# Four heads per attention step, transposed by VectorE into 32-row groups, in a fused attention and two-MoE kernel

## The chip, the cores and the metric

One core of one Trainium2 chip runs the whole program. The metric is the device time of one execution in microseconds (us); lower is better. The engines named below are TensorE (PE in the rows; PEld is its weight load), VectorE (DVE), ScalarE (ACT), GpSimd (POOL) and SyncE (SP), which only issues transfers here.

## The reference

Attention with a sigmoid in place of the softmax, then two feed-forward layers. All data are float32.

```
q, k, v: [4 batches, 12 heads, 448 positions, 64]
scores = q @ k.T / 8 - log(448);  attn = sigmoid(scores);  o = attn @ v
x  = o with heads side by side: [1792 tokens, 768]
x  = silu(x @ w_in) @ w_out                 # w_in 768x2048, w_out 2048x768
h  = x @ w_in2;  g = (a0+a1 h+a2 h^2+a3 h^3) / (1+|b0||h|+|b1|h^2+1e-6)
out = g @ w_out2                            # [1792, 768]
```

## The kernel before

Everything is one program, written in order by hand: each engine works through its own instructions in the order of the code and waits by semaphores for the others. A float32 product is made of three passes in a shorter format: each operand is split into a high part (a copy into that format, by ScalarE) and a low part (the rest, a subtraction by VectorE), and high x high, low x high and high x low are added up in PSUM. The attention comes first and takes the first 158 us; then the two feed-forward layers run, with their own loops, which the change leaves alone but for where the output rows go.

**Attention.** A step `i` is a pair of heads (24 steps, `NPT`); two steps `e` and `o = e+1` make a period, of which there are 12. The 448 keys are three and a half chunks of 128: chunks 0, 1 and 2 of each step are units of their own, and the half chunks of `e` and `o` share the unit `LAST`. For a step, `load_k` and `load_q` bring k and q; q comes in pieces of 128 bytes so that `attn_X`, VectorE's transpose of 32x32 blocks, gives head dimensions on the rows; k is put in order by GpSimd (`mix`) and transposed by TensorE (`attn_T`, four 128x128 transposes against `ident`). `attn_C` splits both: two ScalarE copies, two VectorE subtractions. `attn_QK` makes a unit's scores: three passes (six for `LAST`), each of two matmuls on 64 rows of the array, one for each head of the pair. `attn_S` is the sigmoid, one ScalarE instruction over 896 columns for both heads, out of one of three PSUM pairs of banks (`pairs`), which it gives back. `attn_AV` multiplies by v, two heads in two column halves of the array; the float32 operands are not split here, so each of its matmuls is two instructions. Its sums lie in the PSUM banks `hb[0]` and `hb[1]`, which `attn_E` copies out by VectorE once in a period; the next period's first `attn_AV` into a bank has to wait for that copy.

**What else runs in the attention.** In the same queues weights are converted (`conv(True)`, put at the end of the last quarter of eight periods, by `CONVS`): ScalarE's absolute value (L238), two VectorE operations that wait for it (L239, L240), and in the next quarter two more (`conv_rest`, L243 and L246). From the fourth period on a generator `operands0` makes three operands for the next stage in each period: a ScalarE copy (`split_later`), a GpSimd subtraction for some, and a VectorE subtraction at the next `flush()`.

**The end.** `second2` makes the output in 128-token tiles of 384 columns; `evict` adds up and `store` sends each to HBM in one transfer (the last in two, on two queues).

Of the kernel before, what the change touches and what calls it, by code (L numbers as in the profile page):

```python
# [11 lines left out]
F32 = mybir.dt.float32  # L12
# [35 lines left out]
def attention_moe_moe(ctx: ExitStack, tc: tile.TileContext, q, k, v, w_in1, w_out1, w_in2, w_out2, a, b2, out):  # L48
# [217 lines left out]
    qs, ks, vs = {}, {}, {}  # L266
    ld_p = [None]
    ks_t = []
    LO, HI = slice(0, D), slice(D, 2 * D)
    SQ = 32  # L270

    def rest_of(i):
        return HI if i % 2 else LO

    def load_by_key(src, t, i, eng_hi, eng=nc.sync):
        b, hp = divmod(i, NP)
        at_ = 0
        for part in (LO, HI):
            n = NCH if part == rest_of(i) else NCH - 1
            (eng_hi if part == HI else eng).dma_start(  # L280
                out=t[part, :, : n * D],
                in_=src[b, 2 * hp : 2 * hp + 2, at_ : at_ + n * D].rearrange("h (p c) d -> p h (c d)", c=n),
            )
            at_ += n * D

    def load_k(i):
        if i < NPT:
            ks[i] = ks_t[i % 4]
            load_by_key(k, ks[i], i, nc.scalar if i < 2 else nc.sync)

    def load_q(i):
        if i >= NPT:
            return
        b, hp = divmod(i, NP)
        t = qs[i] = ld_p[0].tile([P, S], F32, tag="qs", name=f"qs_{i}", bufs=3)
        for part in range(2 * D // SQ):
            j, e0 = divmod(part * SQ, D)
            (nc.scalar if i == 0 and part % 2 else nc.sync).dma_start(
                out=t[part * SQ : (part + 1) * SQ, :].rearrange("l (c d) -> l c d", d=SQ),
                in_=q[b, 2 * hp + j, :, e0 : e0 + SQ].rearrange("(c l) d -> l c d", l=SQ),  # L300
            )

    mixed, xq = {}, {}

    def mix(i):
        if i >= NPT:
            return
        t = ks.pop(i)
        u = mixed[i] = ld_p[0].tile([P, 2 * NCH * D], F32, tag="km", name=f"km_{i}", bufs=2)
        dst, src = u.rearrange("p (c h d) -> p h c d", c=NCH, h=2), t.rearrange("p h (c d) -> p h c d", c=NCH)  # L310
        if i:
            nc.gpsimd.tensor_copy(dst, src)
            return
        for h, eng in enumerate((nc.vector, nc.gpsimd)):
            eng.tensor_copy(dst[:, h], src[:, h])

    def load_v(i):
        if i >= NPT:
            return
        vs[i] = ld_p[0].tile([P, 2, NCH * D], F32, tag="vs", name=f"vs_{i}", bufs=4)  # L320
        load_by_key(v, vs[i], i, nc.gpsimd, nc.gpsimd)
# [12 lines left out]
    Q2 = 2 * 2 * S  # L334
    qst = Ring([xa_all[:, i * 2 * S : (i + 1) * 2 * S].rearrange("p (j s) -> p j s", j=2) for i in range(2)])
    k_at = [Q2 + PAD + i * 2 * BK for i in range(3)]
    kst = Ring([xa_all[:, i : i + 2 * BK].rearrange("p (j s) -> p j s", j=2) for i in k_at])

    hb = []
    st, at = {}, {}  # L340
# [7 lines left out]
    rows = (slice(0, D), slice(D, 2 * D))  # L348

    def attn_T(i, p=None):  # L350
        t = mixed.pop(i)
        pk = p if p is not None else pairs.get()
        o = p if p is not None else pk[:, 0, :]
        for c in range(NCH):
            nc.tensor.transpose(o[:, c * P : (c + 1) * P], t[:, c * P : (c + 1) * P], ident)
        return p, pk, o

    def attn_X(i):
        x = xq[i] = ld_p[0].tile([P, S], F32, tag="xq", name=f"xq_{i}", bufs=1)
        nc.vector.transpose(x, qs.pop(i))  # L360

    def attn_C(i, p, pk, o):
        k_, q_ = st["k", i], st["q", i] = kst.get(), qst.get()
        both = ((k_, o[:, :BK]), (q_, xq.pop(i)))
        for x, src in both:
            nc.scalar.copy(x[:, 0, :], src)
# [1167 lines left out]
```

## Time and profile before

| what | us |
|---|---|
| median of 3 runs | 1033.39 (1032.8 to 1034.83) |
| the profiled execution: time | 1035.44 |
| its span, first to last instruction | 1033.7 |
| the attention in it | 0 to 158.14 |
| one attention period (12 of them) | about 12.5 |

The profiled execution is one run; the difference of 1.7 us between its time and its span lies before the first and behind the last instruction. Busy time is the time in which an engine had an instruction running; for TensorE the ends of matmuls are modelled, so that a busy TensorE may still have small gaps.

### The profile page before, as it was taken

The numbers are of one execution on the slowest core, as the hardware profiler recorded it, in microseconds if no ns is written. First come the engines' busy times: TensorE is split into PE (matmuls) and PEld (weight loads), VectorE is DVE, ScalarE is ACT, GpSimd is POOL, SyncE is SP. The second block draws the span as 40 slices with busy tenths as digits, with TensorE's granted clock in tenths as the row PEclk, the third lists the DMA queues.
The fourth block names the chain that finished last, engine by engine and source line by source line (L and its number), as shares of the span: only waits on it lengthen the run. The fifth ranks groups of instructions, "written<-read, shape, count | busy, mean of one in ns | idle before, by whom it ended". The sixth has DMA issues, their size and how long they took to land.

```text
span 1033.7 us, 15953 instructions
## 1 busy us (share of the span) xinstructions
PE 1025.8 (99%) x5568; PEld 894.2 (87%) x5568; DVE 700.8 (68%) x990; ACT 651.7 (63%) x967; POOL 271.3 (26%) x242
## 2 busy tenths in 40 slices
PE   9999999999999999999999999999999999999998
PEld 6555558999999988999988888888999999999998
DVE  4588766878977666354545639889897968655761
ACT  6788786676777666354645668676768866444430
POOL 4335420000000000000000065878958922310000
PEclk9999999999999999999999999999999999999999
DMA  8988777878677766598979734666778869976641
GB/s 173 214 192 205 199 208 255 271 235 277 228 280 246 269 234 226 192 355 302 392 283 378 280 105 152 218 225 205 261 256 301 285 214 298 346 254 204 221 155 54
DMA packets 183504, 249.29 MB, mean 241 GB/s; under 512 B 57280, under 2 KB 136768, under 8 KB 183424
## 3 DMA queue, kind: packets, MB, share of 16 engines
q1 hardware_dynamic: 169504, 224.10, 66.5%
q10 hardware_dynamic: 11152, 17.36, 4.9%
q0 software_dynamic: 2768, 6.82, 2.6%
q8 instruction: 44, 0.72, 0.3%
q14 instruction: 36, 0.29, 0.1%
HBM read 164.60 MB, written 83.62 MB: 240 GB/s over the span
## 4 chain that ended last, share of the span: by engine, by line
PE 75%; DVE 15%; ACT 5%; issue 2%; DMA 2%; POOL 1%; SPq 0%; DVEq 0%; ACTq 0%; POOLq 0%
PE hp L1000 13%; PE acc L578 13%; PE hb L407 7%; PE pair L383 6%; PE acc L725 6%; PE acc L726 6%; PE acc L727 6%; PE hb L1000 5%; PE hb L578 5%; DVE sb L831 3%; DVE sb L829 3%; DVE sb L844 3%; DVE hb L845 3%; ACT sb L826 2%; PE hb L725 2%
## 5 line engine op out<-in xcount | busy, mean ns | idle before, releaser
L725 PE MATMUL acc<-xa_all,woH 128*128 128x512 f32 (+1 forms) x252 | 91.9, 365 | 0.0
L726 PE MATMUL acc<-xa_all,woH 128*128 128x512 f32 (+1 forms) x252 | 91.9, 365 | 0.0
L727 PE MATMUL acc<-xa_all,woL 128*128 128x512 f32 (+1 forms) x252 | 91.9, 365 | 0.0
L398 ACT ACTIVATE sb<-pair,nls 128x896 f32<-128x896 f32 x84 | 80.4, 1011 | 16.1 <-PE pair L383 16.0
L435 POOL TENSOR_TENSOR woL<-wif,woH 128x768 fp32r<-128x768 f32 x9 | 16.5, 1854 | 248.1 <-ACT woH L434 248.1
L827 POOL TENSOR_TENSOR sb<-sb 128x1024 f32<-128x1024 f32 (+1 forms) x32 | 69.7, 2178 | 39.0 <-ACT sb L824 39.0
L407 PE MATMUL hb<-sb,vs 128*64 128x448 f32 (+1 forms) x384 | 73.0, 554 | 0.0
L230 ACT ACTIVATE sb<-sb 128x768 f32<-128x768 f32 x48 | 43.1, 897 | 42.2 <-DMA w1i<-sb 22.7
L578 PE MATMUL acc<-xb,wr 128*128 128x448 f32 x315 | 66.9, 362 | 0.0
L918 POOL TENSOR_TENSOR sb<-sb 128x384 f32<-128x384 f32 (+1 forms) x43 | 52.7, 1231 | 52.4 <-DMA sb<-gk 50.5
L578 PEld LDWEIGHTS acc<-xb,wr 128*128 128x128 f32 x315 | 58.9, 187 | 4.7 <-issue 0.7
L800 PE MATMUL hp<-hx,woL 128*128 128x512 f32 (+1 forms) x168 | 60.7, 362 | 0.0
L798 PE MATMUL hp<-hx,woH 128*128 128x512 f32 (+1 forms) x168 | 60.7, 362 | 0.0
L799 PE MATMUL hp<-hx,woH 128*128 128x512 f32 (+1 forms) x168 | 60.7, 362 | 0.0
L798 PE MATMUL hp<-xa_all,woH 128*128 128x512 f32 (+1 forms) x168 | 60.7, 362 | 0.0
L799 PE MATMUL hp<-xa_all,woH 128*128 128x512 f32 (+1 forms) x168 | 60.7, 362 | 0.0
L800 PE MATMUL hp<-xa_all,woL 128*128 128x512 f32 (+1 forms) x168 | 60.7, 362 | 0.0
L232 DVE TENSOR_SCALAR sb<-sb 128x768 f32<-128x768 f32 x52 | 29.0, 558 | 43.3 <-ACT sb L230 43.0
L824 ACT ACTIVATE sb<-sb,absb 128x1024 f32<-128x1024 f32 (+1 forms) x32 | 36.4, 1139 | 33.5 <-DVE hb L845 33.2
L233 DVE SCALAR_TENSOR_TENSOR sb<-sb 128x768 int32<-128x768 int32 x48 | 46.0, 959 | 13.0 <-ACT sb L231 11.9
L829 DVE TENSOR_TENSOR sb<-hp,sb 128x768 f32<-128x768 f32 (+1 forms) x31 | 33.6, 1084 | 28.9 <-ACT sb L826 28.8
L725 PEld LDWEIGHTS acc<-xa_all,woH 128*128 128x128 f32 x252 | 47.3, 188 | 5.5
(259 smaller groups left out, 2795.0 us busy)
## 6 DMA issues: line engine op xcount, KB each, us to landing
sb<-in_moe_w_in_dram SPq DMA_DIRECT2D x30, 768.0 KB, 7.3
sb<-in_moe_w_out_dram SPq DMA_DIRECT2D x29, 768.0 KB, 6.9
gd<-sb SPq DMA_DIRECT2D x64, 224.0 KB, 3.0
wf<-w0i SPq DMA_DIRECT2D x28, 384.0 KB, 4.1
gk<-sb SPq DMA_DIRECT2D x28, 384.0 KB, 3.6
gk<-sb SPq DMA_DIRECT2D x15, 512.0 KB, 3.1
woL<-gk SPq DMA_DIRECT2D x25, 256.0 KB, 4.9
w1i<-sb SPq DMA_DIRECT2D x16, 384.0 KB, 5.6
```

Of the source, the lines that this page charges most:

```text
L398: nc.scalar.activation(t, p[:, :, :S], AF.Sigmoid, bias=nls, scale=QKSCALE)
L407: nc.tensor.matmul(hb[i_ % 2][j * D : (j + 1) * D, :S], vs[i_][part, j, c * D : (c + 1) * D], t[part, j], start=(c == 0), stop=(c == LAST),)
L578: nc.tensor.matmul(o, w_[:, w], x[:, i_, :], start=first and kk == 0 and n_ == 0, stop=kk == HK - 1 and n_ == 2, skip_group_check=not first,)
L725: nc.tensor.matmul(o, woH[c][:, w], x[:, 0, :w_], start=(c == 0), stop=False)
L726: nc.tensor.matmul(o, woH[c][:, w], x[:, 1, :w_], start=False, stop=False)
L727: nc.tensor.matmul(o, woL[c][:, w], x[:, 0, :w_], start=False, stop=(c == KF - 1))
L798: nc.tensor.matmul(o, wh[:, w], x[:, 0, :wd_], start=first, stop=False)
L799: nc.tensor.matmul(o, wh[:, w], x[:, 1, :wd_], start=False, stop=False)
L800: nc.tensor.matmul(o, wl[:, w], x[:, 0, :wd_], start=False, stop=last)
L827: nc.gpsimd.tensor_tensor(out=q_, in0=q_, in1=a_, op=ALU.mult)
L829: nc.vector.tensor_tensor(out=u1, in0=o, in1=u1, op=ALU.mult)
L1000: nc.tensor.matmul(o, a_, y[:, w_, :], start=kk_ == 0 and n_ == 0, stop=kk_ == HF - 1 and n_ == 2)
```

## The change

The attention takes two of the old steps at once. A step `x` (12 steps, `NQ`) is four heads, A the first two and B the last two. The pieces:

- `load_kq` brings k and q of four heads in one transfer each, 3584 contiguous bytes for every row: a row of SBUF holds 14 consecutive positions of one head, and each head has 32 rows. The order of tokens so becomes a permuted one, the same for all heads; `store` undoes it, with four transfers of 32 rows for each tile where there was one.
- `attn_X` transposes k and q by VectorE, six instructions for a step: for each half of the 64 head dimensions k's 384 and 64 columns and q's 448. Four heads then lie in four groups of 32 rows.
- `attn_C` copies the high parts: k by GpSimd, q by ScalarE. `attn_L` makes the low parts with four VectorE subtractions. TensorE's transposes, `mix` and their PSUM are gone.
- `attn_QK` makes two units at once, one of A and one of B: six rounds (three passes for each half of the head dimensions), each of four matmuls on 32 rows of the array that write four different banks. The half chunks of A and B share one PSUM pair over two turns; a short ScalarE read (`fence`) of it stands between.
- A step is four turns: scores of two units, sigmoids (2, 2, 1, 2 units), then `attn_AV` of units of the turn before (3 or 2 or 1 of them). In the first turn of step `x` the work for `x+1` is done: `attn_X` at its beginning, then `attn_C`, `attn_E` of `x-1`, `attn_L`, and the loads for `x+2`.
- At the end of the attention `hb` is a pool of its own that is closed, and the later pair of banks (`hpair`) is allocated again.

```diff
+    def load_kq(x):
+        if x >= NQ:
+            return
+        b, hq = divmod(x, H // HQ)
+        for nm, src in (("k", k), ("q", q)):
+            t = raw[nm, x] = ld_p[0].tile([P, NB * D], F32, tag="raw", name=f"{nm}_{x}", bufs=3)
+            a_ = src[b, hq * HQ]
+            for eng, part in ((nc.sync, slice(0, P)),) if x else ((nc.sync, LO), (nc.scalar, HI)):
+                n = part.stop - part.start
+                eng.dma_start(
+                    out=t[part, :],
+                    in_=bass.AP(a_.tensor, a_.offset + part.start * NB * D, [[NB * D, n], [1, NB * D]]),
+                )
...
+    KT, QT = wf[1], (s12f, s34f)
+
+    def attn_X(x):
+        if x >= NQ:
+            return
+        src_k, src_q = (raw.pop((nm, x)).rearrange("p (b x) -> p b x", x=D) for nm in "kq")
+        n = LAST * NCH
+        for h in range(2):
+            dims = slice(h * SQ, (h + 1) * SQ)
+            nc.vector.transpose(
+                KT[h][:, P:BK].rearrange("p (c g l) -> p g c l", c=LAST, g=NCH),
+                src_k[:, :n, dims].rearrange("p (g c) x -> p g c x", c=LAST),
+            )
+            nc.vector.transpose(KT[h][:, :D].rearrange("p (b l) -> p b l", l=SQ), src_k[:, n:, dims])
+            nc.vector.transpose(QT[h][:, :S].rearrange("p (b l) -> p b l", l=SQ), src_q[:, :, dims])
+
+    def attn_C(x):
+        if x >= NQ:
+            return
+        (kh, _), (qh, _) = parts[x % 2]
+        for h in range(2):
+            (nc.gpsimd.tensor_copy if x else nc.scalar.copy)(kh[:, h, D:], KT[h][:, :BK])
+            nc.scalar.copy(qh[:, h], QT[h][:, :S])
+
+    def attn_L(x):
+        if x >= NQ:
+            return
+        (kh, kl), (qh, ql) = parts[x % 2]
+        for h in range(2):
+            for src, hi_, lo in ((KT[h][:, :BK], kh[:, h, D:], kl[:, h, D:]), (QT[h][:, :S], qh[:, h], ql[:, h])):
+                nc.vector.tensor_tensor(out=lo, in0=src, in1=hi_.bitcast(F32), op=ALU.subtract)
+
+    last_of = {}
+
+    def attn_QK(x, *units):
...
+        for n, (a_, b_) in enumerate(((0, 0), (1, 0), (0, 1))):
+            for h in range(2):
+                for (s_, c), p in zip(units, ps):
+                    again = (x, c) in last_of
+                    at_ = M0 + c * P if c < LAST else D - s_ * D
+                    for j in range(2):
+                        r = slice((2 * s_ + j) * SQ, (2 * s_ + j + 1) * SQ)
+                        nc.tensor.matmul(
+                            p[:, j, :S],
+                            K[a_][r, h, at_ : at_ + P],
+                            Q[b_][r, h, :],
+                            start=(n == 0 and h == 0 and not again),
+                            stop=(n == 2 and h == 1),
+                            skip_group_check=again,
+                        )
+        for (s_, c), p in zip(units, ps):
+            if c == LAST and (x, c) not in last_of:
+                last_of[x, c] = p
+                nc.scalar.copy(fence, p[0:1, :, 0])
+            else:
+                at[x, s_, c] = p
+
...
-        dst = out[c0 : c0 + P, e0 : e0 + HM]
-        cut = HM // 2
-        if end:
-            nc.sync.dma_start(out=dst[:, :cut], in_=t[:, :cut])
-            nc.scalar.dma_start(out=dst[:, cut:], in_=t[:, cut:])
-        else:
-            nc.sync.dma_start(out=dst, in_=t)
+        for at_ in range(0, P, SQ):
+            b, r = divmod(c0 + at_, S)
+            dst = out[b * S : (b + 1) * S, e0 : e0 + HM].rearrange("(l b) e -> b l e", b=NB)[r // SQ]
+            eng = nc.scalar if end and at_ >= P // 2 else nc.sync
+            eng.dma_start(out=dst, in_=t[at_ : at_ + SQ, :])
 
...
+        A, B_ = 0, 1
+        SCORES = (((A, 0), (B_, 0)), ((A, 1), (B_, 1)), ((A, 2), (B_, LAST)), ((A, LAST), (B_, 2)))
+        READY = (SCORES[0], SCORES[1], ((A, 2),), ((A, LAST), (B_, 2)))
+        BEHIND = (((A, LAST), (B_, 2)), ((A, 0), (B_, 0)), ((A, 1),), ((B_, 1), (A, 2)))
+
+        for n in range(4 * NQ):
+            x, turn_ = divmod(n, 4)
             conv_outs()
+            if turn_ == 0:
+                attn_X(x + 1)
+            attn_QK(x, *SCORES[turn_])
+            attn_S(x, *READY[turn_])
+            of = x if turn_ else x - 1
+            if of >= 0:
+                for u in BEHIND[turn_]:
+                    attn_AV(of, *u)
+            if turn_ == 0:
+                attn_C(x + 1)
+                if of >= 0:
+                    attn_E(of)
+                    load_v(x + 1)
+                attn_L(x + 1)
+                load_kq(x + 2)
             flush()
             conv_rest()
+            if x >= NQ // B and turn_ != 2:
                 next(first_ops, None)
...
```

## Rows read from the trace of the kernel before

**Rows 1.** The page: span, busy time of TensorE, its granted clock in 40 slices
```profile
span 1033.7 us, 15953 instructions
...
PE 1025.8 (99%) x5568; PEld 894.2 (87%) x5568; DVE 700.8 (68%) x990; ACT 651.7 (63%) x967; POOL 271.3 (26%) x242
...
PEclk9999999999999999999999999999999999999999
```

**Rows 2.** Busy time by stretch (instructions), clock, DMA share: two periods, eleven together
```profile
32.43:44.93 12.50, 12.50 (x90) 6.77 (x90) 8.18 (x14) 9.53 (x13) 4.96 (x7) 1.00 1.04 237
82.47:95.09 12.62, 12.52 (x90) 6.80 (x90) 12.24 (x15) 10.30 (x16) 9.67 (x11) 1.00 0.77 195
19.95:158.14 138.19, 138.03 (x973) 73.98 (x973) 97.46 (x142) 109.62 (x150) 53.40 (x73) 1.00 0.84 205
```

**Rows 3.** The chain that ended last: start, length; second period, one whole, the end
```profile
19.95 2.01 PE pair L383 x18
...
43.27 1.65 PE hb L407 x8
44.93 2.01 PE pair L383 x18
46.94 1.82 PE hb L407 x12
48.75 1.41 PE pair L383 x12
50.16 0.59 PE pair L355 x4
50.75 2.40 PE hb L407 x12
...
154.82 3.32 PE hb L407 x20
158.14 9.33 PE acc L578 x45
```

**Rows 4.** Timeline where a period begins, at 82.47: start, length [idle before]
```profile
82.39 1.70 PEld L383 LDWEIGHTS pair<-xa_all 64*128 64x128 f32 x18 [0.70 <-ACT sb L398]
...
82.97 0.58 ACT L440 CAST xb<-xk 128x448 fp32r<-128x448 f32 x1
...
83.44 0.93 ACT L238 ACTIVATE sb<-sb 128x768 f32<-128x768 f32 x1
...
84.26 2.80 ACT L398 ACTIVATE sb<-pair,nls 128x896 f32<-128x896 f32 x3
84.39 0.56 DVE L239 TENSOR_SCALAR sb<-sb 128x768 f32<-128x768 f32 x1
...
84.99 1.38 DVE L240 TENSOR_SCALAR sb<-sb 128x768 int32<-128x768 int32 x1
85.30 0.21 PEld L407 LDWEIGHTS hb<-sb,vs 64*64 64x64 f32 x8 [0.70 <-issue]
...
86.38 1.15 DVE L420 COPY xk<-hb 128x448 f32<-128x448 f32 x2
```

**Rows 5.** Groups of VectorE in 82.47:95.09: count, busy us, mean ns, idle before
```profile
L360 DVE STREAM_TRANSPOSE xq<-qs 128x448 f32<-128x448 f32 x2 | 1.3, 630 | 0.0
L368 DVE TENSOR_TENSOR qx<-xq,qx 128x448 fp32r<-128x448 f32 x1 | 1.2, 1226 | 0.1
```

**Rows 6.** Timeline at the start: the first transpose and the first scores
```profile
6.49 0.65 DVE L360 STREAM_TRANSPOSE xq<-qs 128x448 f32<-128x448 f32 x1 [1.70 <-DMA qs<-in_q_dram]
...
7.79 1.74 PE L383 MATMUL pair<-xa_all 64*128 64x448 f32 x12 [0.15 <-ACT xa_all L366]
```

**Rows 7.** Timeline at the end: the stores of the last three tiles
```profile
1029.02 0.86 SPq L1043 DMA_DIRECT2D out_dram<-sb  x2
...
1030.46 0.33 SPq L1040 DMA_DIRECT2D out_dram<-sb  x1
```

**Rows 8.** DMA issues over the whole run: count, KB each, median us to landing
```profile
wif<-w1i SPq DMA_DIRECT2D x16, 384.0 KB, 5.4
out_dram<-sb SPq DMA_DIRECT2D x27, 192.0 KB, 2.2
```

More of the change, by code (lines that the diff above doesn't have):

```diff
@@ L286, in load_k @@
[L286 to L301, printed above, removed]
@@ L346, in warm @@
             nc.tensor.transpose(p[:, 1, :P], ident, ident)
[L348 to L366, printed above, removed]
-        for x, src in both:
-            nc.vector.tensor_tensor(out=x[:, 1, :], in0=src, in1=x[:, 0, :].bitcast(F32), op=ALU.subtract)
-        if p is None:
-            pairs.put(pk)
-    LAST = NCH - 1
-    def attn_QK(i, c):
-        p = pairs.get()
-        parts = [(i, ((0, 0), (1, 0), (0, 1)))]
-        if c == LAST:
-            parts.append((i + 1, parts[0][1]))
-        turns = [(i_, n) for i_, passes in parts for n in passes]
-        for n, (i_, (a_, b_)) in enumerate(turns):
-            K, Q = st["k", i_], st["q", i_]
+    M0 = P + D
@@ new lines, in attn_S, with attn_AV @@
+    def attn_S(x, *units):
+        for s_, c in units:
+            p = at[x, s_, c]
+            t = f2.get()
+            nc.scalar.activation(t, p[:, :, :S], AF.Sigmoid, bias=nls, scale=QKSCALE)
+            pairs.put(p)
+            at[x, s_, c] = t
+    seconds = {}
+    def attn_AV(x, s_, c):
+        t = at.pop((x, s_, c))
+        for w in (s_,) if c < LAST else (0, 1):
+            part = slice(0, P) if c < LAST else (LO, HI)[w]
+            n = seconds[x, w] = seconds.get((x, w), 0) + 1
@@ L1055, in attention_moe_moe @@
-        qst.put(ld_p[0].tile([P, 2, S], F32R, tag="qx", name="qx"))
-        ld_p[0].tile([P, 16], F32, tag="qxpad", name="qxpad")
-        for i in range(2):
-            load_k(i)
-            load_q(i)
-        for i in range(4):
-            nc.vector.memset(ks_t[i][rest_of(i + 1), :, LAST * D :], 0.0)
+        load_kq(0)
         constants()
-        warm(16)
-        mix(0)
+        open_parts()
+        warm(24)
+        load_v(0)
         attn_X(0)
-        attn_C(0, *attn_T(0, hb[0]))
@@ L1152, in attention_moe_moe @@
+            if at_half == -3:
+                prep_s12(0)
+            if at_half == -1:
+                prep_a22(0)
+            if n == 0:
+                conv_load()
+            if n == 3:
+                conv_load()
+            if n == 4:
+                coefficients()
+            if n == 12:
+                coefficients_abs()
+            if n in CONVS:
+                conv(True)
         for _ in first_ops:
             pass
-        for u in waiting:
-            attn_AV(*u)
-        attn_E(NPT - 2)
@@ L1157, in attention_moe_moe @@
-        attn_E(NPT - 1)
+        for u in BEHIND[0]:
+            attn_AV(NQ - 1, *u)
+        attn_E(NQ - 1)
         flush()
```

251 lines of the change are left out of this document (95 added, 156 removed).

## The prediction

> **What bounds the kernel now.** The page comes first: TensorE has work for 99% of the span and its clock was granted in full in all 40 slices [rows 1]. With an engine so full the question is where its time stands between matmuls, so next comes the table by stretches over the attention: eleven periods and the last one's remainder, 19.95 to 158.14, took 138.19 us with TensorE busy for 138.03, while VectorE (97 us) and ScalarE (110 us) had room and the DMA engines fell from a share of 1.04 to 0.77 without the period getting shorter [rows 2]. So transfers and ScalarE set nothing there; TensorE does. The third view is the chain of waits, which for one period is TensorE alone, one kind of matmul after another [rows 3]. There the reader can take a price list. Scores: 18 matmuls 2.01 us, 12 take 1.41, so a pair of matmuls, side by side on two halves of the rows, costs 0.20, and each group has 0.21 on top for the change of shape. Products with v: 8 instructions 1.65, 12 take 2.40, so 0.19 each and 0.15 on top; the group with the shared half chunk has 12, eight of them on quarters of the array, and takes only 1.82: four small tiles at once cost what two do. Transposes: 0.59 twice a period. The fourth view is the timeline at the start of a period with a weight conversion, where VectorE's order becomes visible [rows 4].
>
> **What TensorE saves.** Removed: the two groups of transposes, 2 x 0.59 = 1.18 a period. The scores keep their streamed columns if four matmuls on 32 rows run side by side: 24 passes of four instead of 24 of two, but in four groups instead of three: 4 x 1.41 = 5.64 against 2.01 + 1.41 + 2.01 = 5.43, since a group of 24 small matmuls is six passes as one of 12 was. The products with v are in four groups: 1.82 + 1.65 + 0.90 + 1.65 = 6.02 (0.90 is 4 x 0.19 + 0.15) against 1.65 + 1.82 + 2.40 = 5.87. A new period is 11.66, an old one about 12.5. From the beginning of the second period to the end of the attention: 11 x 11.66, plus 1.82 for the products left over, is 130.1 against 138.2. That is -8.1 us.
>
> The trace has no 32-row matmul. Its lower bound for a pass of four is the 0.20 of a pair; its upper bound comes from the weight loads, 18 in 1.70 us, 0.094 each [rows 4]: if four loads had to follow each other, a pass would last 0.38, and 288 passes would cost 288 x 0.18 = 52 us. I take 0.20, because pairs already load two weights in one pass and the four quarter tiles cost no more than two halves [rows 3].
>
> **What VectorE gets, and the new wait.** VectorE loses two transposes a period (0.63 each [rows 5]) and gets six: 1792 columns where it had 896. Two operations of 448 columns back to back take 1.15 with 0.62 for one [rows 4], so one adds 0.53; by columns six cost 4 x 0.53 = 2.1, by count 6 x 0.53 = 3.2. Two are only 64 wide, so I take 2.3. The four subtractions stay. Mean load goes from 8.9 to about 10.1 of 11.7: below TensorE's, but the place matters. All six stand at the head of the first turn, before `attn_E`, and the first product with v of the second turn writes `hb[0]`, which `attn_E` has to have copied. Reckoned from the first turn's beginning TensorE comes to that product at 1.41 + 1.82 + 1.41 = 4.64. Where VectorE is free at 0, six transposes end at 2.3, the copy waits for TensorE until about 3.3 at the worst, and nothing is lost. Where a conversion was put at the end of the turn before, VectorE's next two instructions wait for ScalarE's L238, which stands behind two sigmoids and, from the fourth period on, a copy. In the last turn scores end 1.65 before the next period; from there 0.15 to the sigmoid (an estimate from modelled ends), 2 x 0.90 for two sigmoids (three took 2.80 with 1.01 each), 0.47 for the copy (start to start of L440 and L238) and 0.93 for L238 make 1.70 after the new period's beginning. Then L239 and L240, 0.60 + 0.56: 2.86; the transposes: 5.16; the copy of `hb[0]`, 0.62 and a semaphore: 5.84. TensorE stands for 5.84 - 4.64 = 1.2. Seven conversions precede a first turn with transposes: five with the copy (1.2 each), two before it (0.7 each): 7.4. In the old order the copy of `hb` came straight behind L240, at 86.38, and had until 82.47 + 2.01 + 1.82 + 1.41 + 0.59 = 88.3 [rows 3, 4], which is why nothing shows before. Once in these conversions L240 ran 1.38 beside GpSimd; I add 0.8 for one of those. Sum +8.2. Below, it is 0 if the order does not bite; above, 3.2 for the transposes makes every stall 0.9 longer, 14.5 in all.
>
> **ScalarE, GpSimd, PSUM.** ScalarE gives k's high part to GpSimd, two copies less a period, and gets the short read `fence`; GpSimd does two copies as `mix` did. In the tightest turn ScalarE has two sigmoids, two copies of q and one for an operand, 2 x 0.90 + 3 x 0.47 = 3.2, against the turn's 1.41 + 1.82 of TensorE: it keeps up, and costs nothing while q is transposed in time. A pair of PSUM banks is wanted again 1.65 after the scores end, and the first sigmoid gives it back after 1.16: 0.5 of cover. Behind the waiting q copies stand the next sigmoids; in a turn with a conversion they move by the same 1.2 that TensorE stands, so the stall is not paid twice.
>
> **Transfers.** q's 128-byte pieces go, and SyncE issues 6 transfers a period where it issued 12: nothing, since TensorE was full at a DMA share of 1.04 and of 0.77 alike [rows 2]. v now waits for its buffer to the end of the first turn and is wanted a period later: covered by eight microseconds, and k and q of `x+2` likewise.
>
> **The start.** Four heads of k and q are 0.92 MB instead of half of it. A 384 KB load lands after 5.4 [rows 8]; I put q at 6.5, where the first q was before [rows 6]. Then: q's first half 0.65, k's and q's second halves 1.1, four subtractions 2.3, so the last pass of the first scores runs at about 10.7, the sigmoid frees a pair at 12.1, scores to 13.55, products to 15.2, then 1.41 + 0.90 + 1.41 + 1.65: the second period begins at 20.55, before at 19.95 [rows 3]: +0.6, between -1 and +4.
>
> **The stores.** SyncE gets 84 issues more, each some 0.35 (0.86 for two [rows 7]); sixteen at once hold its queue for 6 us, and the loads behind them are asked for 14 units of 1.6 to 2 us ahead, so they cost nothing; if that cover went, 6 us each time. At the very end the last tile's four transfers follow those of two earlier tiles on two queues: the last issue starts about 0.7 later, 48 KB land perhaps 0.2 sooner than 96: +0.5, between 0 and 1.
>
> **Sum.** -8.1 + 8.2 + 0.6 + 0.5 = +1.2. The profiled execution took 1035.44, 2.05 above the median of the runs; against the median the forecast is 1033.4 + 1.2 = 1034.6 us.
>
> **Rivals.** (a) *The conversions do not hold the copies up*: the stall is gone and -7.0 remains, 1026.4 us. For it: VectorE has a fifth of its time free, and five periods have no such stall. Against it: the order of code and the 1.70. It decides where the copy of `hb[0]` ends before 4.64. (b) *VectorE fills up.* A period with conversion and operands asks for 1.16 + 2.3 + 1.1 + 2.3 + 1.6 (three operand subtractions) + 1.8 (L243 and L246, by their 768 columns at 0.53 for 448) = 10.3 alone, but the fullest such period already took it 12.24 of 12.62 [rows 2], because operations beside GpSimd stretch: a subtraction took 1.23 where a like one is 0.62 [rows 5]. With 1.2 more it is 13.4 for 12.9. From there a backlog goes over into the next period's transposes; 0.5 to 1.2 in five periods is +3 to +6, 1039 us. The Trainium skill (GPSIMD Engine Reference, section 1, Specifications) says that GpSimd shares its SBUF access with VectorE's instructions that have two SBUF inputs. By that rule k's subtractions, which read PSUM and SBUF before and SBUF twice now, become open to it too, and the sum would be at this rival's upper end; the trace agrees for q's, at 1.23 against 0.62. (c) *TensorE's clock.* In the start TensorE has only six passes between 6.4 and 12.1. If its granted clock fell there to the lower level (1.2 GHz, half), the next scores and products, 1.41 + 1.65, would double: +3, 1037.6. Against it: nothing before shows a fall, but nothing before stood so long either. (d) *Passes of four are slower than pairs.* With 0.06 more, a third of the way to the bound above, 288 passes cost 17 us and the kernel ends at 1052; with loads in a row, 1086. For it: no row has four 32-row matmuls. Against it: quarter tiles at the price of halves. The Trainium skill (TensorE: Matmul & The Clock Gate, Part 3, Packing small matmuls) gives 3.07 times for four row tiles instead of four; by that a pass would be 4 x 0.20 / 3.07 = 0.26 and the cost 17.5.
>
> **How the numbers follow.** Forecast 0.37, its own range 1031 to 1037; (a) 0.27; (b) 0.20; (c) 0.08; (d) 0.08. A measurement of this kernel can tell about 0.2%, 2.1 us, from no change. Faster: (a) and the lower edge of the forecast, 0.30. Same: most of the forecast and the weakest of (a) and (b), 0.30. Slower: (b), (c), (d) and the forecast's upper edge, 0.40. The range takes half of (a) in and leaves out (d): 1027 to 1043.
>
> **What would show it.** The chain should have no transposes and a period without conversion of 11.7. The wait list should show TensorE's products with v waiting for VectorE's copies of `hb`, some 1.2 in five periods and 0.7 in two; if that line is short, (a) holds. Score groups of 24 should take 1.41; 1.75 or more is (d). The granted clock of 0 to 20 us decides (c). VectorE's busy time above 12.5 in a period, with waits of scores on its low parts, is (b). The forecast is wrong in its main step if the periods after a conversion are no longer than the others.

## The result, and the profile after

The changed kernel takes 1043.51 us, median of four runs (1041.82 to 1046.35); the kernel before, run beside it, takes 1034.11. The ratio is 1.0095, with a 95% interval of 1.0068 to 1.0122: slower by 9.4 us. The forecast was 1034.6 with a range of 1027 to 1043, so it lies outside, if only just. The profiled execution took 1041.82, the fastest of the four, against 1035.44 before: +6.4 us are there to be read in the trace. The other 3 us of the medians are not: 1.7 because the changed kernel's profiled execution is its fastest, 1.3 because that of the kernel before lies above its median.

The page of the changed kernel, to be laid beside [rows 1]:

```profile
span 1040.0 us, 16921 instructions
...
PE 1018.2 (98%) x6048; PEld 886.0 (85%) x6048; DVE 709.6 (68%) x1033; ACT 644.0 (62%) x957; POOL 269.2 (26%) x250
...
PEclk8999999999999999999999999999999999999999
...
DMA packets 140387, 249.34 MB, mean 240 GB/s; under 512 B 17296, under 2 KB 90960, under 8 KB 140304
```

The clock's first slice of 26 us is no longer full. The table of stretches shows where (each row: stretch, length, busy time of the engines, then granted clock, DMA share and GB/s):

```profile
6.00:8.00 2.00, 0.36 (x4) 0.12 (x2) 0.00 (x0) 0.62 (x1) 0.51 (x1) 1.00 0.99 280
8.00:10.00 2.00, 0.00 (x0) 0.00 (x0) 0.90 (x2) 0.22 (x1) 0.56 (x1) 0.81 0.82 165
10.00:18.00 8.00, 6.46 (x50) 4.07 (x52) 6.57 (x15) 4.85 (x8) 2.87 (x5) 0.50 0.72 181
...
25.63:37.31 11.68, 11.68 (x131) 5.92 (x130) 3.52 (x6) 7.70 (x11) 3.30 (x6) 1.00 0.46 120
37.31:49.58 12.27, 11.79 (x132) 5.93 (x130) 8.51 (x16) 8.59 (x12) 3.45 (x6) 1.00 0.52 131
```

From 6.4 to the first scores at 10.40 TensorE had nothing to do; its clock fell in that time, at 9.2, and was 0.50, the lower level, up to 19.5; of the eight microseconds in the table TensorE was busy for 6.46. The chain shows what that costs, the first three lines at the lower level and the last at the full one:

```profile
11.56 2.62 PE pair L409 x20
...
15.22 2.61 PE pair L409 x22
17.82 2.48 PE hb L440 x8
20.31 1.41 PE pair L409 x15
```

The second period begins at 25.63, where it began at 19.95. The last two rows of the table are the attention's steady state: a period without a conversion ahead of it takes 11.68, with TensorE busy throughout; one with a conversion 12.27, and later, with an operand's copy in ScalarE's queue as well, about 12.7. What stands between is in the list of TensorE's waits from 0 to 165 (total, times, longest), which before held nothing but 1.4 for the start and one wait of 0.2. L383 makes q's high part, L454 and L457 copy `hb`, and L420 is `fence`; the 1.4 of the start is still there and left out here, with one wait of 0.7 for a sigmoid:

```profile
PE pair L409 <- ACT xa_all L383: 4.5, 2, 4.0
PE hb L440 <- DVE xk L454: 3.9, 5, 1.1
PE hb L440 <- DVE sb L457: 2.8, 3, 0.9
PE pair L409 <- ACT ident L420: 1.8, 1, 1.8
```

And the chain of waits through one such period, where [rows 3] had TensorE alone:

```profile
61.23 1.00 ACT sb L428
62.23 0.45 ACT xb L474
62.69 0.80 ACT sb L238
...
63.51 0.57 DVE sb L239
...
64.10 0.56 DVE sb L240
64.66 0.49 DVE wf L370
...
66.39 0.53 DVE sf L375
66.91 0.52 DVE xk L454
...
67.48 1.72 PE hb L440 x8
```

Sigmoid, an operand's copy, the conversion's L238, its two VectorE operations, six transposes (2.25 us), the copy of `hb[0]`, and only then the product with v. Behind the start the attention has no transposes on TensorE any more.

**The ledger of the two profiled executions** (after less before): start of the second period +5.68; from there to the first matmul behind the attention (at 165.30 and 158.07) 139.67 against 138.12, +1.55; first feed-forward layer -1.62; from its end to the last matmul +0.04; from the last matmul to the end of the span +0.73. The sum is +6.38. The +0.04 is itself a sum: laid matmul by matmul beside the kernel before, the changed one gains another 2.0 up to 915 and loses 2.1 in one place at 920, to which experiment 4 comes.

### The profile page after: what moved, and what is told of

Read it like the earlier page. It is cut to its first block, busy times and chain, and to the rows that moved or that the text cites. A ratio compares the mean times of both kernels' runs of the same rounds, so it can differ in the third digit from the quotient of the medians.

```text
span 1040.0 us, 16921 instructions
## 1 busy us (share of the span) xinstructions
PE 1018.2 (98%) x6048; PEld 886.0 (85%) x6048; DVE 709.6 (68%) x1033; ACT 644.0 (62%) x957; POOL 269.2 (26%) x250
## 2 busy tenths in 40 slices
DMA packets 140387, 249.34 MB, mean 240 GB/s; under 512 B 17296, under 2 KB 90960, under 8 KB 140304
## 4 chain that ended last, share of the span: by engine, by line
PE 64%; DVE 18%; DMA 6%; ACT 6%; issue 4%; POOL 2%; SPq 1%; ACTq 0%; DVEq 0%; POOLq 0%
PE acc L612 14%; PE hp L1034 9%; PE acc L759 6%; PE acc L760 6%; PE acc L761 6%; PE hb L612 5%; PE pair L409 4%; PE hb L440 4%; PE hbpair L1034 3%; DVE sb L865 2%; DVE sb L878 2%; DVE sb L863 2%; DVE hbpair L879 2%; PE hb L759 2%; PE hb L760 2%
## 5 line engine op out<-in xcount | busy, mean ns | idle before, releaser
L440 PE MATMUL hb<-sb,vs 128*64 128x448 f32 (+1 forms) x384 | 76.4, 562 | 6.7 <-DVE xk L454 3.9
L440 PEld LDWEIGHTS hb<-sb,vs 128*64 128x64 f32 (+1 forms) x384 | 19.4, 136 | 42.5 <-issue 22.3
L233 DVE SCALAR_TENSOR_TENSOR sb<-sb 128x768 int32<-128x768 int32 x48 | 46.0, 959 | 13.1 <-ACT sb L231 11.7
```

The costliest lines, as they stand in the source:

```text
L440: nc.tensor.matmul(hb[w][j * D : (j + 1) * D, :S], vs[x][part, 2 * w + j, c * D : (c + 1) * D], t[part, j], start=(n == 1), stop=(n == NCH),)
```

## The experiments

The theory after the result: the start lost 5.7 us by q's late landing and by the fall of the clock that follows it, and the conversions' stalls took back what TensorE saved. The rivals were that VectorE is simply too full, that the stores cost time in the middle, and that the start is one of the two causes alone.

**1. Copies first.** `hb` is copied ahead of the transposes; the splitting for `x+1` goes to the second turn.

```diff
             if turn_ == 0:
-                attn_X(x + 1)
...
-                attn_C(x + 1)
                 if of >= 0:
                     attn_E(of)
                     load_v(x + 1)
-                attn_L(x + 1)
+                attn_X(x + 1)
                 load_kq(x + 2)
+            if turn_ == 1:
+                attn_C(x + 1)
+                attn_L(x + 1)
```

> In the changed kernel's trace the seven periods behind a conversion are 0.6 to 1.2 us longer than 11.68, and one more and a wait of 1.9 in the third turn add to 9.2 us in all. Theory order: these waits come from the six transposes standing ahead of the copies of hb in VectorE's queue. With the copies first, and the high and low parts in the second turn, the periods behind a conversion go to 11.7 to 11.9, the attention ends 6 to 9 us earlier (before 159.5 instead of 165.4), and the time falls by as much, to about 1036. Rival full: VectorE has more work than the period has time; then the waits only move, to the scores' low parts or to the fence, and the attention ends less than 3 us earlier. The start (second period at about 25.6) stays in both.

Measured: 1039.67 us, ratio 1.0052 (1.0032 to 1.0071). No product with v waits for a copy of `hb` any more. Six periods in a row from 26.20 to 96.40 take 11.68 to 11.72, conversions or not; the second of them, which took 12.27 in the changed kernel:

```profile
37.88:49.60 11.72, 11.72 (x131) 5.93 (x130) 9.18 (x16) 8.48 (x12) 4.12 (x6) 1.00 0.51 163
```

Five of the six have a conversion ahead of them, so these five stalls were the order's and not VectorE's amount of work. Then one of 15.5: scores wait for low parts (1.6 in two waits) behind a VectorE subtraction that took 3.71, and the granted clock is 0.50 from 99.7 to 103.1. Attention ends at 161.65 instead of 165.30, 3.7 us earlier where 6 to 9 were expected: the late stalls, with VectorE behind, are the rival's.

**2. Conversions two turns later.** The other way to part the two.

```diff
-        CONVS = (7, 11, 15, 19, 23, 31, 35, 43)
+        CONVS = (9, 13, 17, 21, 25, 33, 37, 45)
```

> The same conversions, each put two turns later (end of the second turn), and nothing else moved: the transposes still stand ahead of the copies of hb, but the conversion's two VectorE instructions, which wait for ScalarE, no longer stand ahead of the transposes. Theory order: the waits for the copies of hb vanish as in the first experiment, 6 to 8 us. Rival full: the same amount of VectorE work, so the waits stay or move, less than 3 us. A wait of the fence or of the sigmoids in the third turn, at most 0.5 each, would be new, since the conversion's ScalarE instruction now stands before the fence.

Measured: 1042.22 us, ratio 1.0069 (1.0054 to 1.0084). The list of waits of this kernel, 0 to 165:

```profile
PE pair L409 <- ACT xa_all L383: 3.6, 2, 2.9
PE pair L409 <- ACT ident L420: 2.2, 1, 2.2
PE hb L440 <- DVE sb L457: 1.8, 2, 1.2
```

The line for `xk` is gone, and the six periods from 25.64 to 95.89 take 11.68 to 11.76. So both orders remove the first five stalls, by different means. Of the next three one is shorter than in the changed kernel and two are longer: 12.96, 12.33 and 15.6 (there 12.67, 12.71 and 14.57), the last with VectorE busy for 13.08 of it and the clock at 0.50 from 133.0 to 136.4, behind a wait of 2.2 for `fence`. The attention ends at 162.0, 3.3 us earlier.

**3. The start, four times.** *q alone*: two raw buffers instead of three, so that k and q of the second step are asked for only when the first are transposed, and v of the first step held until then as well.

```diff
-            t = raw[nm, x] = ld_p[0].tile([P, NB * D], F32, tag="raw", name=f"{nm}_{x}", bufs=3)
+            t = raw[nm, x] = ld_p[0].tile([P, NB * D], F32, tag="raw", name=f"{nm}_{x}", bufs=2)
...
+        attn_X(0)
+        nc.gpsimd.tensor_copy(ident[0:1, 2:4], QT[0][0:1, 0:2])
         load_v(0)
-        attn_X(0)
```

> One part of the start alone: the first v and the second k are asked for only after the first q is transposed. In the changed kernel q's second half landed at 9.08, its first at 6.25. Theory late q: both halves land by about 6.5, the first scores begin at 7.5 to 8 instead of 10.4, and the second period begins at 21.5 to 23.5 instead of 25.6. Rival clock: if TensorE's granted clock still falls to 0.5 in the start, at least 2 us of that are not won, and the second period begins later than 23. Rival bandwidth elsewhere: v or the second k come so late that the second turn or the second period waits for them; then nothing is won.

*Warmer*: TensorE transposes `ident` 44 times ahead of the first scores.

```diff
-        warm(24)
+        warm(44)
```

> The other part of the start alone: 44 warming transposes instead of 24, so that TensorE is busy from 1.4 to about 10.5; loads as in the changed kernel. Theory clock: the granted clock stays at 1.0, the scores and products between 11.5 and 20 take 1.4 and 1.65 instead of 2.6 and 2.5, and the second period begins at 22.5 to 23.5 instead of 25.6; the runs lie closer together than the 1041.8 to 1046.4 of the changed kernel, with a mean clock of 1.0. Rival: the clock falls all the same, in the gaps between 10.5 and 14, and less than 1 us is won.

*Both, with filling*: q alone (the copy that holds v back now writes into another small tile), 32 transposes ahead, four after each of the first five passes of scores and six behind the last.

```diff
+                if fill_now and n + h < 3:
+                    warm(fill_now)
...
-        warm(24)
+        warm(32)
...
-            attn_QK(x, *SCORES[turn_])
+            attn_QK(x, *SCORES[turn_], fill_now=0 if n else 4)
+            if n == 0:
+                warm(6)
```

> Both parts of the start together: first v and second k asked for after the first q, 32 warming transposes, and more of them between the first scores' passes and behind them, so that TensorE never stands long. Theory start: the granted clock stays at 1.0 throughout, and the second period begins at 20 to 22 instead of 25.6, so the attention ends 3.5 to 5.5 earlier. Rival loads: the second q and the first v come too late in any order (2.3 MB are wanted in the first 14 us), and the second period does not begin before 23.

*Two raw buffers only*: the first line of *q alone*, with v asked for at once.

> The changed kernel with two raw buffers instead of three: k and q of the second item are asked for only when VectorE has transposed k and q of the first, and v of the first item is still asked for at once. In the changed kernel the ACT half of q landed 7.74 us after its issue, first scores at 10.40, second period at 25.63. Theory (the second item's k is what makes q late): the ACT half lands about 5.5 to 6 us after its issue, first scores near 8.5, second period near 23.5 to 24.5, and v is there for the first products, unlike in the run that held v back. Rival (v's many short pieces make it late): it still lands 7 us or more after its issue and the second period starts at 25 or later. In either case the end moves by no more than that: 1041 to 1043 against 1043.5.

| kernel | us, ratio (interval) | q's ACT half lands after | first scores | second period | granted clock |
|---|---|---|---|---|---|
| changed | 1043.51, 1.0095 (1.0068 to 1.0122) | 7.74 | 10.40 | 25.63 | 0.50 from 10 to 18 |
| two raw | 1041.86, 1.0074 (1.006 to 1.0088) | 6.31 | 8.97 | 24.29 | 0.50 from 8 to 18 |
| q alone | 1045.24, 1.0099 (1.008 to 1.0118) | 5.16 | 7.83 | 24.54 | 0.50 from 10 to 18 |
| warmer | 1045.33, 1.0104 (1.0089 to 1.0119) | 7.01 | 9.68 | 25.06 | 0.50 from 12.5 to 19.3 |
| both, filled | 1043.64, 1.0091 (1.0076 to 1.0105) | 5.62 | 8.29 | 24.48 | 1.00 up to 136 |

The landing is read off the head of the chain of waits. In the changed kernel:

```profile
1.34 7.74 DMA q<-in_q_dram
```

With two raw buffers, and with q alone:

```profile
1.34 6.31 DMA q<-in_q_dram
```

```profile
1.35 5.16 DMA q<-in_q_dram
```

These are the same 224 KB, issued at the same time, in one execution each, and executions differ: with the loads of the changed kernel six traces have 6.98 to 7.74 (this one, experiments 1, 2 and 4, *warmer*, and the twelve subtractions of experiment 6), with two raw buffers three have 5.85 to 6.31, with v held back too three have 5.16 to 5.64. The three groups do not overlap, so both loads beside it delay q: k of the second step (448 KB) by about 1 us, v of the first (eight transfers) by about half of one. But earlier scores did not bring the whole of it. With v held back its first product waited for v (0.4), and in both versions the clock fell to 0.50 all the same. More transposes ahead only moved the fall. With filling the clock stayed at 1.00:

```profile
10.00:18.00 8.00, 7.57 (x68) 4.78 (x70) 3.46 (x8) 3.01 (x5) 4.89 (x10) 1.00 0.90 209
```

But the first six passes, with their filling, lasted from 8.29 to 13.9 and ate what the clock gave. So both causes are there and neither alone makes the start short; the last version of experiment 6, with two raw buffers, a clock of 1.00 and less filling, has its first scores at 8.81 and the second period at 22.20, where two raw buffers alone, with scores at 8.97, have it at 24.29: the clock is worth about 2 us there.

The whole times do not follow the start: *q alone* and *warmer* begin the second period earlier than the changed kernel and have higher medians, with overlapping intervals. What a start is worth is read off the traces here, not off the medians. In *both, filled* the wait of 1.8 for `fence` near 135 was followed by a fall of the clock that the changed kernel has not, and the attention ends at 165.73, no earlier.

**4. One store for a tile.** As before the change; this kernel leaves out putting the output's tokens back in order.

```diff
...
-        for at_ in range(0, P, SQ):
...
-            eng.dma_start(out=dst, in_=t[at_ : at_ + SQ, :])
+        dst = out[c0 : c0 + P, e0 : e0 + HM]
+        cut = HM // 2
+        if end:
+            nc.sync.dma_start(out=dst[:, :cut], in_=t[:, :cut])
+            nc.scalar.dma_start(out=dst[:, cut:], in_=t[:, cut:])
+        else:
+            nc.sync.dma_start(out=dst, in_=t)
```

> The changed kernel with the stores of before: one transfer for a tile, so the permuted order of the tokens is not undone in the output. In the changed kernel TensorE stands 1.8 us near 918 (2.75 in another run of its family, with the granted clock at 0.5 after it), behind loads that SyncE issued late after four stores in a row, and its last stores end about 0.7 later. Theory stores: without them that wait is gone, the stretch from the first matmul of the next stage to the end of the span is 2 to 4 us shorter than in the changed kernel's family (871 to 874 to the last matmul, 4.6 behind it), the tail is 3.9, the median falls by 2 to 4 and the runs lie closer together. Rival: the wait has another cause, and the time does not change by more than 1.

Measured: 1040.64 us (1039.03 to 1041.54), ratio 1.0062 (1.0047 to 1.0077): 2.9 less than the changed kernel, and its runs lie closer together. In the list of waits of the changed kernel, from 800 on, the first row is a wait that the kernel before has not:

```profile
PE hp L1034 <- ACT sb L1053: 1.8, 1, 1.8
```

With one store for a tile the longest there is the following (before it was 0.6):

```profile
PE hp L1034 <- DVE sb L865: 0.9, 1, 0.9
```

The changed kernel's chain ahead of it shows how the issues get there:

```profile
903.38 0.29 SPq L1075
...
903.72 0.41 SPq L1075
904.19 0.41 SPq L1075
904.64 0.42 SPq L1075
...
907.57 5.33 DMA woL<-gk
912.98 0.63 ACT hx L990
913.63 0.70 DVE hx L991
914.34 0.23 SPq L984
914.67 5.16 DMA wif<-wt
919.83 0.06 ACT woH L464
...
920.23 0.86 ACT sb L1053 x2
```

These four stores hold SyncE for 1.7 us, and of the eleven issues from 899.1 to 905.1 ten are stores; the loads asked for behind them land late; ScalarE waits for one of them (L464) ahead of the eviction L1053, and TensorE for the eviction. In the kernel with 44 transposes the same wait was 2.8, and the granted clock then was 0.50 from 923.8 to 927.2. The other traces bear the stores out as the cause: laid matmul by matmul beside the kernel before, each of the eight versions of the changed kernel whose stores there all go through SyncE loses 1.6 to 4.4 us at this place, and neither this one nor the three of experiment 6 whose stores are shared with GpSimd lose anything there. In the two profiled executions the store edit is worth only 1.2 us (0.36 up to the last matmul, 0.85 behind it, 4.55 against 3.7), because the changed kernel had gained 1.7 more than this one on the way there, for a reason that was not looked at; the medians say 2.9.

**5. The kernel before with `hb` as two tiles.** The change gives the two `hb` banks tiles of their own until the attention's end; this does that alone.

```diff
-        hb_all = hb_p.tile([P, 2, 512], F32, tag="hb", name="hb")
-        hb.extend(hb_all[:, j] for j in range(2))
-        hpair.append(hb_all)
+        hb.extend(fixed("hb", 2, [P, 512], F32, hb_p))
...
         ps_s.close()
+        hb_s.close()
         ps_p = ctx.enter_context(tc.tile_pool(name="ps2", bufs=1, space=PSUM, reuse_waits="tile"))
+        hpair.append(ps_p.tile([P, 2, 512], F32, tag="hbpair", name="hbpair"))
...
```

> The kernel before with one part of the change alone: hb as two tiles in a pool that is closed, and the pair allocated again. In the changed kernel the first feed-forward stage is 1.6 us shorter than before, at three places where before TensorE's products into hb waited for ScalarE's reading of the other half. Theory two tiles: those waits go, and the kernel is 1.0 to 1.6 us faster than before, about 1033. Rival: they went because everything came later against the transfers; then the time is that of before, within 0.5.

Measured: 1034.03 us, ratio 1.000 (0.9991 to 1.0009). The kernel before has this wait in its first feed-forward layer, and this kernel and the changed one have not:

```profile
PE hb L578 <- ACT sb L597: 0.8, 2, 0.4
```

From the attention's end to the last matmul it takes 870.1 instead of 871.77 us, so the -1.62 of the ledger is this edit's. But the whole is no faster: over all runs of this comparison the median span is 0.85 shorter (1031.55 against 1032.40) and what lies outside the span 0.6 longer (2.38 against 1.80), and in its profile the stretch behind the last matmul is 5.3 instead of 3.8. Why the end takes it back isn't known.

**6. What is left of the stalls, and a version that is faster.** The late stalls all have long VectorE operations ahead of them. VectorE's timeline in the changed kernel, and GpSimd's of the same stretch:

```profile
93.49 0.67 DVE L391 TENSOR_TENSOR xa_all<-wf,xa_all 128x512 fp32r<-128x512 f32 x1
94.08 0.61 DVE L391 TENSOR_TENSOR xa_all<-sf,xa_all 128x448 fp32r<-128x448 f32 x1
94.62 3.37 DVE L391 TENSOR_TENSOR xa_all<-wf,xa_all 128x512 fp32r<-128x512 f32 x1
```

```profile
95.18 3.82 POOL L516 TENSOR_TENSOR xk<-xk,xk 128x448 f32<-128x448 f32 x3
```

A subtraction of 0.67 takes 3.37 beside GpSimd's of the operands. So these twelve were given to VectorE:

```diff
-        nc.gpsimd.tensor_tensor(out=o, in0=i0, in1=i1, op=ALU.subtract)
+        nc.vector.tensor_tensor(out=o, in0=i0, in1=i1, op=ALU.subtract)
```

> The changed kernel with the twelve subtractions of GpSimd at L516 (1.31 us each on GpSimd) done by VectorE instead. In the changed kernel seven of VectorE's two-input operations between 69 and 139 took 1.57 to 3.37 us where 0.61 to 0.96 is usual, some 10.3 us too long in all, each beside such a subtraction of GpSimd. Theory (VectorE's two-input operations stand while GpSimd subtracts): all of VectorE's operations go back to 0.61 to 0.96, at a price of twelve times 0.61, 7.3 us; the period from 87.25, which was 1.2 too long without a sigmoid's conversion ahead of it, comes back to 11.7 to 12.0, and attention ends 1 to 2 us earlier. Rival (the backlog is VectorE's amount of work, whoever does the subtractions): the sum of VectorE's busy time over attention rises, and the periods from the seventh on are as long as before or longer.

Measured: 1048.01 us, ratio 1.0144 (1.0124 to 1.0165), the slowest of all. The first half of the theory held; the groups of VectorE's subtractions from 25 to 172 in this kernel:

```profile
L516 DVE TENSOR_TENSOR xk<-xk,xk 128x448 f32<-128x448 f32 x12 | 7.3, 620 | 0.1
...
L391 DVE TENSOR_TENSOR xa_all<-wf,xa_all 128x512 fp32r<-128x512 f32 x10 | 6.8, 679 | 0.0
```

679 ns where the changed kernel's mean was 1271: with GpSimd's subtractions out of the way these are no longer stretched. But the second half, that attention then ends sooner, was wrong: it ends at 172.57, and the rival, periods as long as before or longer, is right: three of them take 15.1 to 16.7. A ScalarE copy that reads such a difference (L474) now waits for VectorE's whole queue, the short read `fence` stands behind it, and TensorE behind that, as the list of waits has it:

```profile
PE pair L409 <- ACT ident L420: 7.0, 3, 2.3
```

Behind two of these three waits the granted clock fell to 0.50 as well.

Three versions then put the edits together, with half of each tile's stores issued by GpSimd. The first has copies first, conversions three turns later, and the start *both, filled*:

```diff
-            eng = nc.scalar if end and at_ >= P // 2 else nc.sync
+            eng = (nc.scalar if end else nc.gpsimd) if at_ >= P // 2 else nc.sync
...
-        CONVS = (7, 11, 15, 19, 23, 31, 35, 43)
+        CONVS = (10, 14, 18, 22, 26, 34, 38, 46)
```

> All together: the copies of hb ahead of the transposes, high and low parts in the second turn, conversions three turns later (end of the third turn), the start of the run before, and half of each tile's stores issued by GpSimd. If order, start and stores are the three causes, the periods are 11.7 to 11.8 throughout, the attention ends at 151 to 154 against 158.1 before, and the time is 1026 to 1031, faster than both kernels. If VectorE is simply full, waits of scores for low parts remain and it ends no earlier than 157.

Measured: 1035.87 us, ratio 1.0018 (1.0008 to 1.0028), where 1026 to 1031 was expected; the second period at 23.49, six periods of 11.68 to 11.72, then one of 13.1 and a last one of 16.1, where ScalarE waits 2.73 for weights that land in a buffer given back late. The second mends that and the start (two raw buffers, v at once, three transposes behind each of the first three passes, not two as the expectation has it):

```diff
+            if turn_ == (0 if x + 1 == NQ - 1 else 1):
+                attn_C(x + 1)
+                attn_L(x + 1)
```

> The combined version once more, with its two late stalls and its start mended: copies of hb ahead of the transposes; the next item's casts and low parts in the second turn, but for the last item in the first, so that the weights that land in the same buffers are asked for in time; conversions three turns later; two raw buffers, v at once; 32 transposes ahead of the first scores, three each behind the first two passes and six behind the sixth; half of the stores issued by GpSimd. Theory: second period at 22 to 23 (23.49 in the first combined version), periods of 11.7 but for one of 13 near 94 to 107, the last one 12 to 13 instead of 16.1, attention ends at 154 to 156, 1031 to 1033 us, so faster than the kernel before by 1 to 3 us. Rival (the stalls only move, and the gain is given back in the stage behind, as with the kernel before and two tiles for hb): 1034 to 1036, no faster than the kernel before.

Measured: 1035.62 us, ratio 1.0013 (1.0004 to 1.0022), the rival's 1034 to 1036. Second period at 21.92; but a sigmoid now stands behind the last step's copies for 2.2, and the attention ends at 157.29. The third takes that back and moves the steps that read those weights instead:

```diff
-            if turn_ == (0 if x + 1 == NQ - 1 else 1):
+            if turn_ == 1:
...
-            if at_half == -5:
+            if at_half == -4:
...
-            if at_half == -3:
+            if at_half == -2:
```

> The second combined version with its last stall taken out: the casts and low parts of the last item stay in the second turn, as for the others, so that the second turn's sigmoid is not queued behind them (2.16 us at 138 in the second combined version); the steps that read the weights landing in the same buffers come one turn later instead (in the first combined version ScalarE waited 2.73 us for them at 143). Theory: the period from 128.9 takes 11.7 to 12.5 instead of 14.9, attention ends at 154 to 155.5 (157.3), the span is 1029 to 1030.5 and the median 1031.5 to 1033.5, faster than the kernel before by 1 to 3 us. Rival (the stalls only move): attention ends after 156.5 and the median is 1034 to 1036.

Measured: 1031.87 us (1030.15 to 1035.59, 12 runs) against 1034.61 for the kernel before beside it: ratio 0.9982, interval 0.9970 to 0.9994. It beats the kernel before by a little, 0.06 to 0.3%, and the changed one by 11.6 us by the medians, which were not taken side by side. Its table of stretches:

```profile
22.20:33.89 11.69, 11.69 (x130) 5.88 (x128) 6.24 (x12) 7.68 (x11) 4.47 (x8) 1.00 0.68 207
92.41:105.51 13.10, 12.15 (x132) 5.79 (x130) 12.65 (x24) 9.19 (x14) 4.15 (x7) 1.00 0.77 224
...
129.17:141.45 12.28, 11.78 (x131) 5.93 (x130) 10.75 (x20) 8.27 (x12) 3.41 (x6) 1.00 0.72 205
```

The attention ends at 154.95, 3.1 earlier than in the kernel before. In the second row GpSimd's subtractions still show: ahead of it, at 87.90, a VectorE subtraction took 3.58 beside them, VectorE then had no gap up to the copy of `hb` at 97.80, and TensorE waited 0.9 for that copy.

## Why the prediction was wrong, step by step

- **The start, "+0.6, between -1 and +4": the step that failed.** It measured +5.7. Two terms were mis-sized in it. q was put at 6.5, by the first q of the kernel before and the 5.4 of loads of 384 KB [rows 8], whose stretch from 533 to 617 had a DMA share of 0.74; the changed kernel's first nine microseconds had 0.93, and q's second half landed at 9.08, 2.6 later. The landings of experiment 3 show that it was v and k of the second step, issued from 0.7 us behind it on. And the sum took every matmul at the full clock: the second scores took 2.6 instead of 1.41 and the products behind them 2.5 instead of 1.65, 2.0 together. About 0.5 more lies between q's landing and the second scores, where the first scores ran at the lower clock too. The 2.0 was rival (c), priced at 3 and given a chance of 0.08; it came together with the late q, not in place of it. From its third turn on the start ran as computed: 5.39 to the second period, forecast 5.37. (The 0.50 is the clock's lower level, 1.2 GHz; TensorE had been without work since 6.36 when it fell, at 9.2.)
- **TensorE saves 8.1: right.** A period without stalls takes 11.68, forecast 11.66. A group of 24 small matmuls takes 1.41 to 1.42, so a pass of four costs the 0.20 of a pair, and rival (d) is out. The estimate of 0.26 from the 3.07 of the Trainium skill (TensorE: Matmul & The Clock Gate, Part 3, Packing small matmuls) is not borne out by these rows, for passes that stream 448 columns.
- **The stalls, +8.2: right in mechanism and size, with two more behind them.** The seven periods exceed 11.68 by 0.59 and 0.56 (forecast 0.7) and by 1.02 to 1.21 in the other five (forecast 1.2), 6.5 in all. The chain itself comes out: in the period from 61.82 L238 ends 1.66 after its beginning (forecast 1.70), the transposes 5.09 (5.16), and the product with v starts at 5.66 (5.84). Rival (a) is refuted by that, and experiments 1 and 2, which make the first five of these periods 11.7, show the order as the cause. Besides these, 0.99 in a period without a conversion and 1.87 in a third turn: the chain at the latter runs L457, four low parts, L479, GpSimd's L516 (1.72), a ScalarE copy, `fence`. That is rival (b), VectorE's backlog beside GpSimd, at 2.9 instead of its 3 to 6, and added to the forecast's case, not instead of it. (VectorE's free time, "a fifth" there, is a seventh by the prediction's own 10.1 of 11.7.) By the Trainium skill (GPSIMD Engine Reference, section 1, Specifications) k's subtractions would become open to GpSimd; they did, at 1271 ns in a mean where 679 is undisturbed.
- **The stores: +0.5 at the end was right (+0.73); "they cost nothing" before it was not.** There is a wait of 1.8 at 920, and 2.1 us are lost there; leaving the edit out gives 2.9 in the medians. The text had looked at how far ahead loads are asked for, not at a ScalarE eviction queued behind a copy that needs one of them.
- **Transfers, ScalarE, PSUM at nothing: right behind the start.** Packets under 512 bytes fell from 57280 to 17296, with no gain in time to be seen.
- **Not seen: -1.6 by the two `hb` tiles**, an edit that the prediction did not price at all; alone it does not shorten the time.

The size of the miss: by the profiled executions the forecast was +1.2 and the result +6.4, of which the start is 5.1. That the rest nearly comes out is partly luck: 1.1 more stalls than forecast and the stores' 2.1 stand against 1.6 and 2.0 that were won where nothing was forecast. The remaining 3 us of the medians no kept trace shows. The other three executions of the changed kernel had mean granted clocks of 0.994, 0.993 and 0.992 where the profiled one had 0.995, so they spent 2 to 6 us more at the lower level (an estimate from these means); experiment 4, without the stores, points at the wait at 920, but where those falls were is open.

## What to carry to other kernels

A start is a stage with its own limits: count every transfer that is issued before the first matmul, not the one that is waited for, and reckon what the first matmuls cost at the lower clock if they come late or thinly. A load's landing is taken from rows with the same company, and a stall's price from what else stands in the queue behind it. When several sound terms cancel, as -8.1 and +8.2 did here, the sum is decided by the small ones, so rivals that can happen at once should be added up and not only weighed one against the other.

## What the hardware showed

- A VectorE subtraction with two SBUF inputs was held up by more than one GpSimd operation: 3.37 us instead of 0.67, across two of GpSimd's three subtractions and into the third, and 2.3 beside a single one of 1.17, though it had started 0.6 before it. In the first combined version one took 3.59, while transposes of 0.53 to 0.60 beside GpSimd's subtractions there were not lengthened.
- The granted clock fell not only in the start but also within a full stream of matmuls, and the length of the last wait did not decide it. It fell behind the wait of 2.8 at 920 (*warmer*), but also behind waits of 1.8 (experiment 2 at 920, *both, filled* at 135) and behind two of 0.9 and 0.7 (experiment 1 near 99); it did not behind the changed kernel's 1.8 at 920 and at 137, nor behind 2.0 at 918 in experiment 1 and one of 2.3 in the kernel of the twelve subtractions.
- Filling the gaps with transposes of `ident` held the clock at 1.00 through the start; 44 of them ahead of the scores, and none in the gaps, did not.
